# Cross attention and a three-way maxout layer: the order of work rewritten as three lists, with transposes by transfer, G in runs and a test of the sums

## The chip, the cores and the metric

The kernel runs on one core of a Trainium2 chip. The metric is the device time of one execution in microseconds (us). Three runs of the kernel before took 165.41, 166.38 and 168.26 us; their median is 166.38. The profile is of one execution, and its times are counted from its first instruction.

## The reference

`x` holds 8 batches of 8 heads, 512 rows and 64 columns; `state` has 32 rows for each batch and head. All inputs and the output are float32.

```python
scores  = softmax(x @ state.T / 8);  xread = scores @ state      # 512 rows per head
scores2 = softmax(state @ x.T / 8);  sread = scores2 @ x         # 32 rows per head
t = concat([xread, sread], axis=2)        # 544 rows per batch and head
t = t.transpose(0, 2, 1, 3).reshape(8 * 544, 512)                # heads side by side
h = max(t @ w1, t @ w2, t @ w3)           # w: 512 x 768
out = h @ w_out                           # 768 x 512
```

The reference takes each row's maximum off before the exponential. The softmax is the same without it as long as no exponential or sum leaves the range of the number type.

## The kernel before

Matmuls are in bf16 and sums in float32. `xread` is never formed. For each batch the kernel computes G, the product of the block of states and the weights (`g_cols`, L239, copied from PSUM at L245), so that layer 1 is `a @ G` (`x_maxout`, L260): `a` holds the softmax weights. G has 2,304 columns for each of two head parities, computed in six slices of 384, one per block `m` of 128 hidden columns.

Per batch the steps are these. `load_x` (L69) loads x on POOL's DMA queue and casts it to bf16. x is transposed on PE, 16 matmuls of 128 columns (`x_transpose`, L150, copied at L153), or by a DMA transpose on SyncE's queue (`x_transpose_dma`, L157). `scores` multiplies (L171) and takes the exponential on ACT (L176), with no maximum taken off. `softmax` sums (L183) and inverts (L185) on DVE and multiplies on POOL (L186). `a` is transposed on PE (`a_transpose`, L197, L198) or by a DMA (`a_transpose_dma`, L202). `sread` (L216) multiplies the same exponentials with x, 32 matmuls whose right side is 64 columns of x and 64 columns of ones that stand behind x, 128 columns in all, so that the sum of each row comes with the product; its result is transposed by a DMA (L224). Layer 1 makes three products per block (L260), copies the first on ACT (L264) and takes the maxima on DVE (L267, L268). Layer 2 (`ffn_out`, L285) makes four groups of 128 rows per batch; ACT copies each (L292) and POOL's or SyncE's queue stores two at a time (L301).

PSUM has two pools: four single banks (tag `pw`: three for each layer-1 group, one for each layer-2 group, and the transposes) and two double ones (tag `two`: slices of G and scores).

The order of each engine is the order in which the code is written; nothing reorders it. Batches 0 and 1 have a part written out by hand, with `keep_busy` matmuls (L116) while the first data come. From batch 2 on, `slots` attaches to each of the six layer-1 blocks of batch b the steps of batch b+1 and the layer-2 groups that are pending. x of batches 0 to 3 and `a` of batches 0 to 2 are transposed on PE; for later batches both are transposed by transfer, and x is loaded two batches before its layer 1.

Of the kernel before, what the change touches and what calls it, by code (L numbers as in the profile page):

```python
# [8 lines left out]
F32 = mybir.dt.float32  # L9
BF16 = mybir.dt.bfloat16  # L10
AX = mybir.AxisListType
AF = mybir.ActivationFunctionType


@with_exitstack
def kernel(
# [10 lines left out]

# [19 lines left out]
    wpool = ctx.enter_context(tc.tile_pool(name="weights", bufs=1))  # L50
# [3 lines left out]


    def load_st(k, eng):
        eng.dma_start(
            out=st_f[k],
            in_=state[2 * k:2 * k + 2].rearrange("b h n d -> (b h n) d").rearrange("(p t) d -> p t d", t=4))

    st_f = [data.tile([128, 4, D], F32, name=f"stf{k}") for k in range(B // 2)]
    load_st(0, nc.sync)


    x_sb = [data.tile([128, XW + D], BF16, name=f"x{b}") for b in range(B)]
    xv = [t[:, 0:XW].rearrange("p (h j d) -> p h j d", j=J, d=D) for t in x_sb]
# [6 lines left out]
    def x0_heads(g):  # L73
        return x[0].rearrange("(s g) (p j) d -> g p s (j d)", g=2, j=J)[g]

    x0_sb = x_sb[0][:, 0:XW].rearrange("p (s g jd) -> g p s jd", g=2, s=HS)
    x0_f = data.tile([128, HS, J * D], F32, name="x0f")
    nc.sync.dma_start(out=x0_f, in_=x0_heads(0))
    zero = const.tile([128, 512], BF16, name="zero")
    nc.vector.memset(zero, 0.0)  # L80
    ident = const.tile([128, 128], BF16, name="ident")
    make_identity(nc, ident)
    nc.gpsimd.dma_start(out=x0_sb[1], in_=x0_heads(1))
    for b in range(B):
        nc.gpsimd.memset(x_sb[b][:, XW:XW + D], 1.0)

    chunks = ((0, 1), (1, 3), (3, 6))
    w_sb = [wpool.tile([128, HS, 3, (m1 - m0) * 128], BF16, name=f"w{m0}") for m0, m1 in chunks]
    wout_sb = wpool.tile([128, NM, d_model], BF16, name="wout")

    def load_w(c):
        m0, m1 = chunks[c]
        for i, w in enumerate((moe_w1, moe_w2, moe_w3)):
            nc.gpsimd.dma_start(  # L94
                out=w_sb[c][:, :, i, :],
                in_=w.rearrange("(kk p) f -> p kk f", p=128)[:, :, m0 * 128:m1 * 128])

    def w_cols(m):
        c = [m0 <= m < m1 for m0, m1 in chunks].index(True)
        f = (m - chunks[c][0]) * 128  # L100
        return w_sb[c], slice(f, f + 128)

    load_w(0)
    bds = [data.tile([128, 2, H, 2, Ns], BF16, name=f"bd{k}") for k in range(B // 2)]
    nc.vector.memset(bds[0], 0.0)
    load_x(1)
    load_w(1)

    warm = const.tile([128, 1], F32, name="warm")
    nc.scalar.activation(out=warm, in_=zero[:, 0:1], func=AF.Exp, scale=1.0)  # L110
    ats = data.tile([128, B, HS, Ns], BF16, name="ats")

    def keep_busy(n):
        p = pp.tile([128, 1024], F32, tag="two", name="idle")
        for _ in range(n):
            nc.tensor.matmul(p[:, 0:512], zero[:, 0:128], zero, start=True, stop=True)  # L116

# [4 lines left out]
    st = [data.tile([128, 4, 2, D], BF16, name=f"st{k}") for k in range(B // 2)]  # L122

    def states_cast(k, cast):
        cast(out=st[k], in_=st_f[k].unsqueeze(2).to_broadcast((128, 4, 2, D)))

    def states(k, copy):

        p = pp.tile([128, 4, 128], BF16, tag="pw", bufs=4, name="pt")
        for t in range(4):  # L130
            nc.tensor.transpose(p[:, t, :], st[k][:, t].rearrange("p c d -> p (c d)"), ident)  # L131
        for c in range(2):
            r = slice(64 * c, 64 * c + 64)
            copy(out=bds[k][r, :, :, c, :].rearrange("p b h (q t) -> p (b h) q t", t=4),  # L134
                 in_=p[r].rearrange("p t (k q) -> p k q t", q=8))


    xT, e, a, aT, G, ht, osb = {}, {}, {}, {}, {}, {}, {}

    def new(d, b, shape, name, bufs=2):  # L140
        d[b] = work.tile(shape, BF16, tag=name, bufs=bufs, name=name)

    def x_transpose(b, g, copy):

        if g == 0:
            new(xT, b, [128, H, 2, 128], "xT")
        p = pp.tile([128, HS, 2, 128], BF16, tag="pw", bufs=4, name="pxt")
        for s in range(HS):
            for jj in range(2):
                nc.tensor.transpose(  # L150
                    p[:, s, jj, :],
                    xv[b][:, 2 * s + g, 2 * jj:2 * jj + 2, :].rearrange("p j d -> p (j d)"), ident)
        copy(out=xT[b].rearrange("p (s g) j t -> p g s j t", g=2)[:, g], in_=p)  # L153

    def x_transpose_dma(b):
        new(xT, b, [128, H, 2, 128], "xT")
        nc.sync.dma_start_transpose(out=xT[b].rearrange("p h j t -> p (h j) t"), in_=x_sb[b][:, 0:XW])  # L157

    def scores(b, g0, g1):
        n = g1 - g0  # L160
        if g0 == 0:
            new(e, b, [128, J, 2, HS, Ns], "e")
        if n == 2:
            p = pp.tile([128, J, n, HS, Ns], F32, tag="two", name="ps")
        else:
            p = pp.tile([128, J, n, HS, Ns], F32, tag="pw", bufs=4, name="psh")
        for jj in range(2):
            for g in range(g0, g1):
                for s in range(HS):
                    h = 2 * s + g  # L170
                    nc.tensor.matmul(  # L171
                        p[:, 2 * jj:2 * jj + 2, g - g0, s, :], xT[b][:, h, jj, :],
                        bd(b, h).rearrange("p c n -> p (c n)"),
                        start=(g == g0 and s == 0 and (n == 2 or jj == 0)),
                        stop=(g == g1 - 1 and s == HS - 1), skip_group_check=True)
        nc.scalar.activation(out=e[b][:, :, g0:g1], in_=p, func=AF.Exp, scale=scale)  # L176

    def softmax(b, g0, g1, mul):
        n = g1 - g0
        if g0 == 0:  # L180
            new(a, b, [128, J, 2, HS, Ns], "a")
        den = work.tile([128, J, n, HS], F32, tag=f"den{n}", name="den")
        nc.vector.reduce_sum(out=den, in_=e[b][:, :, g0:g1], axis=AX.X)  # L183
        rden = work.tile([128, J, n, HS], F32, tag=f"rden{n}", name="rden")
        nc.vector.reciprocal(out=rden, in_=den)  # L185
        mul(  # L186
            out=a[b][:, :, g0:g1].rearrange("p j g s n -> p j (g s) n"),
            in0=e[b][:, :, g0:g1].rearrange("p j g s n -> p j (g s) n"),
            in1=rden.rearrange("p j g s -> p j (g s)").unsqueeze(3).to_broadcast((128, J, n * HS, Ns)))

    def a_transpose(b, g, copy):

        if g == 0:
            new(aT, b, [128, J, 2, 128], "aT", bufs=3)
        p = pp.tile([128, J, 128], BF16, tag="pw", bufs=4, name="pat")
        for j in range(J):
            nc.tensor.transpose(p[:, j, :], a[b][:, j, g].rearrange("p s n -> p (s n)"), ident)  # L197
        copy(out=aT[b][:, :, g, :], in_=p)  # L198

    def a_transpose_dma(b):  # L200
# [4 lines left out]
    late = []  # L205

    def sread(b):

        p = pp.tile([128, 2, 2, D], F32, tag="pw", bufs=4, name="psr")
        for j in range(J):  # L210
            for g in range(2):
                for s in range(HS):
                    xj = xv[b][:, 2 * s + g, j, :]
                    both = bass.AP(xj.tensor, xj.offset,
                                   (xj.ap[0], (XW - ((2 * s + g) * J + j) * D, 2), (1, D)))
# [4 lines left out]
        rd = work.tile([128, 2, 1], F32, tag="rd", name="rd")  # L220
        nc.vector.reciprocal(out=rd, in_=p[:, :, 1, 0:1])
        sr = work.tile([128, 2, D], BF16, tag="sr", bufs=B, name="sr")
        nc.vector.tensor_mul(out=sr, in0=p[:, :, 0, :], in1=rd.to_broadcast((128, 2, D)))
        late.append(lambda: nc.sync.dma_start_transpose(  # L224
            out=ats[:, b].rearrange("p s n -> p (s n)"), in_=sr.rearrange("p g d -> p (g d)")))


    copies_due = []

    def g_cols(b, ms, copies=(nc.scalar.copy, nc.scalar.copy), defer=(False, False)):  # L230

        for m, copy, wait in zip(ms, copies, defer):
            if m == 0:
                new(G, b, [128, 2, NM * 384], "G", bufs=3)
            w, f = w_cols(m)
            p = pp.tile([128, 2, 512], F32, tag="two", name="pg")
            for s in range(HS):
                for g in range(2):
                    nc.tensor.matmul(  # L239
                        p[32 * s:32 * s + 32, g, 0:384].rearrange("p (i f) -> p i f", i=3),  # L240
                        bd(b, 2 * s + g)[64 * g:64 * g + 64, g, :], w[64 * g:64 * g + 64, s, :, f],
                        start=True, stop=True, tile_position=(64 * g, 32 * s))

            def place(m=m, p=p, copy=copy):
                copy(out=G[b][:, :, m * 384:(m + 1) * 384], in_=p[:, :, 0:384])  # L245

            if wait:
                copies_due.append(place)
            else:
                place()  # L250


    def maxout(b, m, n, lhs, rhs, nk):
        if m == 0:
            new(ht, b, [128, NM, n], "ht", bufs=4)
        pw = []
        for i in range(3):
# [196 lines left out]
```

## Time and profile before

| | |
|---|---|
| median of three runs | 166.38 us (165.41 to 168.26) |
| span of the profiled execution | 164.5 us |
| PE, weight loads, DVE, ACT, POOL busy | 149.7, 70.9, 96.0, 99.1, 44.0 us |
| first layer-1 matmul, end of the last matmul | 13.6, 160.3 us |
| layer 1 of x, 288 matmuls (L260) | 71.2 us |
| layer 2 (L285) | 47.9 us |
| copies of G on ACT (L245), 48 | 36.5 us, 0.805 each |
| copies of layer 1 on ACT (L264), 48 | 28.3 us, 0.590 each |
| maxima on DVE (L267, L268), 48 each | 32.6 and 33.0 us |

The profile gives the profiled execution's own time as its span alone; the three timed runs lie 0.9, 1.9 and 3.8 us above it. PE's busy time counts a modelled end for each matmul; sums of what groups occupy are lower than its column. In a line of the chain stand start, duration and what ran; in a line of groups, what is written and read, the count, the busy time and the mean in ns.

### The profile page before, as it was taken

Reading aid. Unit: us, or ns where it says so; the run is one execution under the profiler, and the core shown is the slowest. Engines: PE = TensorE matmul, PEld = TensorE weight load, DVE = VectorE, ACT = ScalarE, POOL = GpSimd, SP = SyncE. Lnnn points to the kernel's source line nnn. Section 1 sums busy time; section 2 is a strip of 40 time slices with the busy share of each in tenths; the row PEclk is TensorE's granted clock in tenths of the full one; section 3 lists DMA queues with packets and bytes.
Section 4 is the critical chain, followed back from the end, with each engine's and each line's share of the span. In section 5 each row is a group of like instructions: output and inputs, shape, how many; then the busy total and the mean of one; then the engine's idle time right before and its main releaser. Section 6 shows DMA issues by size and latency. Waiting matters only on the chain.

```text
span 164.5 us, 3569 instructions
## 1 busy us (share of the span) xinstructions
PE 149.7 (91%) x1432; PEld 70.9 (43%) x1449; DVE 96.0 (58%) x162; ACT 99.1 (60%) x158; POOL 44.0 (27%) x64
## 2 busy tenths in 40 slices
PE   7658699988999999999999999999999999999990
PEld 2425243533445444434344434444444466665430
DVE  4675777889418553665548464865586455585001
ACT  3355578366896678853876688648755853333440
POOL 8975550106150601081016101410141010100140
PEclk9999999999999999999999999999999999999999
DMA  4999999800039999269992989460306030030373
GB/s 132 195 174 199 204 200 248 122 7 0 0 120 130 144 256 198 53 116 145 277 193 87 133 187 104 162 191 14 128 0 195 8 130 0 0 132 0 128 235 148
DMA packets 31824, 20.94 MB, mean 127 GB/s; under 512 B 17184, under 2 KB 29344, under 8 KB 31808
## 3 DMA queue, kind: packets, MB, share of 16 engines
q0 software_dynamic: 15632, 15.08, 46.3%
q1 hardware_dynamic: 16176, 5.64, 18.5%
q8 instruction: 11, 0.18, 0.5%
q14 instruction: 5, 0.04, 0.1%
HBM read 15.20 MB, written 8.91 MB: 147 GB/s over the span
## 4 chain that ended last, share of the span: by engine, by line
PE 63%; DVE 11%; ACT 10%; DMA 6%; POOL 4%; issue 4%; DVEq 0%; ACTq 0%; POOLq 0%
PE pw L260 34%; PE po L285 20%; DMA x<-in_x_dram 4%; PE pg L239 4%; DVE den L183 4%; DVE t L267 3%; ACT e L176 3%; ACT G L245 3%; DVE ht L268 3%; PE ps L171 2%; ACT t L264 2%; PE psr L216 2%; POOL w L94 1%; DMA out_dram<-osb 1%; POOL a L186 1%
## 5 line engine op out<-in xcount | busy, mean ns | idle before, releaser
L260 PE MATMUL pw<-aT,G 128*128 128x512 bf16 x288 | 71.2, 379 | 3.6 <-ACT G L245 1.8
L267 DVE TENSOR_TENSOR t<-t,pw 128x512 bf16<-128x512 bf16 (+1 forms) x54 | 35.1, 650 | 41.6 <-ACT t L264 40.0
L285 PE MATMUL po<-wout,ht 128*128 128x512 bf16 x188 | 47.9, 380 | 0.8
L260 PEld LDWEIGHTS <-G 128*128 128x128 bf16 x288 | 26.7, 98 | 36.2 <-issue 5.1
L245 ACT CAST G<-pg 128x768 bf16<-128x768 f32 x48 | 36.5, 805 | 8.0 <-PE pg L239 7.6
L264 ACT CAST t<-pw 128x512 bf16<-128x512 f32 (+1 forms) x54 | 30.5, 566 | 14.1 <-PE pw L260 12.6
L268 DVE TENSOR_TENSOR ht<-t,pw 128x512 bf16<-128x512 bf16 (+1 forms) x54 | 35.5, 658 | 5.6
L292 ACT COPY osb<-po 128x512 f32<-128x512 f32 x33 | 19.4, 587 | 21.2 <-PE po L285 20.7
L285 PEld LDWEIGHTS <-ht 128*128 128x128 bf16 x204 | 18.4, 98 | 23.6 <-issue 4.7
L301 POOL DMA_DIRECT2D out_dram<-osb x14 | 7.8, 559 | 70.2 <-ACT osb L292 70.2
L186 POOL TENSOR_TENSOR a<-e,rden 128x1024 bf16<-128x1024 bf16 (+1 forms) x8 | 14.4, 1800 | 33.4 <-DVE rden L185 19.8
L239 PE MATMUL pg<-w,bd 64*32 64x384 bf16 x384 | 13.0, 328 | 1.1 <-DMA w<-in_moe_w_dram 1.1
L183 DVE TENSOR_REDUCE den<-e 128x32 f32<-128x1024 bf16 (+1 forms) x9 | 9.9, 1095 | 2.6 <-ACT e L176 2.6
L176 ACT ACTIVATE e<-ps 128x1024 bf16<-128x1024 f32 x7 | 7.2, 1024 | 5.8 <-PE ps L171 5.8
L260 PE MATMUL pw<-ats,w 128*128 128x256 bf16 x72 | 8.8, 273 | 0.0
L239 PEld LDWEIGHTS <-bd 64*32 64x32 bf16 x384 | 3.6, 89 | 11.7 <-issue 11.7
L260 PEld LDWEIGHTS <-w 128*128 128x128 bf16 x72 | 7.0, 98 | 2.1
L94 POOL DMA_DIRECT2D w<-in_moe_w_dram x9 | 6.8, 770 | 0.0
L69 POOL DMA_DIRECT2D x<-in_x_dram x7 | 6.7, 957 | 0.0
L150 PE MATMUL pxt<-ident,x 128*128 128x128 bf16 x64 | 4.4, 219 | 2.2 <-DMA x<-in_x_dram 1.1
L134 ACT COPY bd<-pt 64x512 bf16<-64x512 bf16 x6 | 3.5, 580 | 4.2 <-PE pt L131 4.1
L171 PEld LDWEIGHTS <-xT 128*128 128x128 bf16 x128 | 4.7, 98 | 2.4 <-DVE xT L153 0.8
(42 smaller groups left out, 63.4 us busy)
## 6 DMA issues: line engine op xcount, KB each, us to landing
out_dram<-osb POOLq DMA_DIRECT2D x14, 512.0 KB, 3.7
x<-in_x_dram POOLq DMA_DIRECT2D x7, 512.0 KB, 9.0
w<-in_moe_w_dram POOLq DMA_DIRECT2D x3, 384.0 KB, 10.3
w<-in_moe_w_dram POOLq DMA_DIRECT2D x3, 256.0 KB, 8.2
wout<-in_moe_w_out_dram POOLq DMA_DIRECT2D x1, 768.0 KB, 16.4
x0f<-in_x_dram SPq DMA_DIRECT2D x1, 512.0 KB, 4.0
out_dram<-osb SPq DMA_DIRECT2D x1, 512.0 KB, 2.7
out_dram<-osb SPq DMA_DIRECT2D x2, 256.0 KB, 2.2
```

Source lines behind the costliest of these rows:

```text
L94: nc.gpsimd.dma_start(out=w_sb[c][:, :, i, :], in_=w.rearrange("(kk p) f -> p kk f", p=128)[:, :, m0 * 128:m1 * 128])
L176: nc.scalar.activation(out=e[b][:, :, g0:g1], in_=p, func=AF.Exp, scale=scale)
L183: nc.vector.reduce_sum(out=den, in_=e[b][:, :, g0:g1], axis=AX.X)
L186: mul(out=a[b][:, :, g0:g1].rearrange("p j g s n -> p j (g s) n"), in0=e[b][:, :, g0:g1].rearrange("p j g s n -> p j (g s) n"), in1=rden.r ...
L239: nc.tensor.matmul(p[32 * s:32 * s + 32, g, 0:384].rearrange("p (i f) -> p i f", i=3), bd(b, 2 * s + g)[64 * g:64 * g + 64, g, :], w[64 * ...
L245: copy(out=G[b][:, :, m * 384:(m + 1) * 384], in_=p[:, :, 0:384])
L260: nc.tensor.matmul(p[:, 0:n], lhs(i, k), rhs(k), start=(k == 0), stop=(k == nk - 1))
L264: nc.scalar.copy(out=t0[:, 0:n], in_=pw[0][:, 0:n])
L267: nc.vector.tensor_max(t1[:, 0:n], t0[:, 0:n], pw[1][:, 0:n])
L268: nc.vector.tensor_max(ht[b][:, m, :], t1[:, 0:n], pw[2][:, 0:n])
L285: nc.tensor.matmul(p, ht[b][:, m, j * 128:(j + 1) * 128], wout_sb[:, m, :], start=(m == 0), stop=(m == NM - 1))
L292: nc.scalar.copy(out=o[:, j, :], in_=p)
```

## The change

Each step becomes a small function with a short name, and the order is three lists of such names: one for batches 0 to 2, one that is run for batches 2 to 6, and one for the rest. A number is a batch (in the second list relative to the round's), a letter the engine that copies or the queue (D DVE, A ACT, P POOL, S SyncE). `l1` is layer 1's matmuls, `m0` its copy, `m1` its maxima, `l2` layer 2, `l2c` its copy, `so` a store, `sc`, `ex`, `sum`, `wt` scores to softmax weights, `g`/`gc` a slice of G and its copy, `gr`/`grc` a run and its copy, `xtd`, `atd`, `srt` DMA transposes of x, `a` and the state read, `lx`, `lw`, `lst` loads.

- x of batches 2 to 7 and `a` of batches 2 to 7 are transposed by DMA on SyncE's queue; batches 0 and 1 stay on PE, and are begun together.
- G of batches 2 to 7 is computed in runs of 512 columns (one of 256), in G's own order of columns, instead of slices per block; weights are one tile, loaded in twelve pieces instead of nine.
- For batches 2 to 7 POOL copies x into a tile with a column of ones between heads (`pad`), and the state read takes 65 columns instead of 128.
- All sums are kept (`seen`). At the end DVE tests that they lie between 1e-18 and 1e18, a matmul adds up the answer over partitions, each engine reads it into a register and branches: if the test fails, all is computed again with the row maximum taken off. With the given inputs the branch goes past this code, which is 4,147 instructions long.
- The last layer-2 group is made in two halves of 256 columns, stored by SyncE's and ACT's queues; the states' rows are stored by two transfers instead of eight.

```diff
+FIRST = """
+    ident; clr 0; zero; lx 1; lst 0 A; lxg 0 1; busy 5; stc 0 D; busy 4; clr 3; lw 1 2 1; stt 0; lx0 S;
+    cx0 D; warm; xt 0 0; stp 0 A; xt 1 0; xtc 0 0 A; sc 0 0; lw 1 2 0; lw 0 1 1; xt 1 1; xones 0; ex 0 0;
+    xtc 1 0 D; sc 1 0; sum 0 0; xtc 1 1 A; xt 0 1; xtc 0 1 D; lw 1 2 2; lw 0 1 2; sc 0 1; sc 1 1; ex 1 0;
+    lw 0 1 0; ex 0 1; g 1 1; ex 1 1; lw 2 4 2; gc 1 1 A; lw 2 4 1; lst 1 A; g 0 0; wt 0 0 P; lw 2 4 0;
+    sum 1 0; wt 1 0 P; sum 0 1; wt 0 1 P; at 1 0; at 0 0; sum 1 1; lw 4 6 0; wt 1 1 D; gc 0 0 A; at 0 1;
+    atc 0 0 D; atc 0 1 D; g 1 0; g 0 1; atc 1 0 D; gc 1 0 A; stc 1 P; lw 4 6 1; xones 1; at 1 1; lw 4 6 2;
+    atc 1 1 A; clr 2; lx 2; l1 0 0; lst 2 P; l1 1 0; m0 0 0; gc 0 1 A; g 0 3; g 1 2; m0 1 0; l1 0 1; sr 0;
...
+    stt 3; srs 2; l1 1 5; l2 0 2; l2 0 0; m0 1 5; stp 3 A; gr 2 0 512; gr 2 1792 2304; gr 2 1024 1280;
+    sum 2 -; grc 2 1280 1792 A; xtd 3; l2 0 1; l2c 0 2 A; grc 2 1024 1280 A; l2c 0 1 A; stc 2 D; stt 2;
+    grc 2 512 1024 D; m1 1 5; grc 2 0 512 D; wt 2 - P; atd 2; l2c 0 0 D; so 0 2 4 A; grc 2 1792 2304 D;
+    stp 2 D; so 0 0 2 P;
+"""
+EACH = """
+    lx 2; sc 1 -; l1 0 0; l2 -1 2; l1 0 1; m0 0 0; l2 -1 0; l2c -1 2 A; xtd 2; gr 1 1024 1280; gr 1 0 512;
+    m1 0 0; m0 0 1; gr 1 512 1024; ex 1 -; l1 0 2; l2c -1 0 A; grc 1 1024 1280 A; m1 0 1; sum 1 -;
+    grc 1 512 1024 A; l2 -1 1; l1 0 3; m0 0 2; wt 1 - P; l1 0 4; atd 1; gr 1 1792 2304; l2c -1 1 A; m1 0 2;
+    pad 1; m0 0 3; grc 1 0 512 A; m0 0 4; gr 1 1280 1792; sr 1; m1 0 3; l2 -1 3; m1 0 4; l1 0 5;
+    grc 1 1792 2304 A; grc 1 1280 1792 A; srs 1; m0 0 5; l2c -1 3 D; m1 0 5; so -1 2 4 P; srt -2;
+    so -1 0 2 S;
+"""
+LAST = """
+    srt 5; srt 6; srt 7; l1 7 0; l1 7 1; l2 6 0; l2 6 1; m0 7 0; m0 7 1; m1 7 0; l1s 0; l1 7 3; m0 s 0;
...
+    l2c s 1 A; sos 1 S; l2c 7 3 A; l2 7 0; so 7 3 4 S; l2c 6 2 A; l2c 7 1 D; look; l2c 7 0 A; so 6 2 4 S;
+    so 7 0 2 S; l2 s 0; l2c s 0 A; sos 0 S; flag; l2p 7 2 0 256; l2p 7 2 256 512; l2pc 7 2 0 256 D;
+    l2pc 7 2 256 512 A; sop 7 2 0 256 S; sop 7 2 256 512 A;
+"""
...
+    def pad(b):
+        xp[b] = work.tile([128, HS, J, 2 * D + 2], BF16, tag="xp", name="xp")
+        nc.gpsimd.memset(xp[b][:, :, :, D:D + 1], 1.0)
+        v = xv[b].rearrange("p (s g) j d -> p g s j d", g=2)
+        for g in range(2):
+            nc.gpsimd.tensor_copy(out=xp[b][:, :, :, g * (D + 1):g * (D + 1) + D], in_=v[:, g])
...
+    def g_run(b, c0, c1):
+        new_g(b)
+        n = c1 - c0
+        if n > 256:
+            p = two_banks([128, 2, 512], F32, "pg")
+            ps = [p[:, g] for g in range(2)]
+        else:
+            p = None
+            ps = [bank([128, 512], F32, "pgh") for _ in range(2)]
+        g_mm(b, lambda s, g: ps[g][32 * s:32 * s + 32, 0:n],
+             lambda v: v.rearrange("p i f -> p (i f)")[:, c0:c1])
...
+    perform(FIRST)
+    for b in range(2, B - 1):
+        perform(EACH, b)
+    perform(LAST)
...
+    bad = nc.values_load(flag[0:1, 0:1], min_val=0, max_val=1,
+                         skip_runtime_bounds_check_because="flag is the result of a comparison")
+    with tc.If(bad != 0):
+        for b in range(B):
...
```

## The prediction

> **What bounds the kernel now.** I read the busy shares first, then the chain that ended last, then stretches of the span, last the DMA queues. Shares, clock, and the queue that loads instructions:
>
> ```profile
> PE 149.7 (91%) x1432; PEld 70.9 (43%) x1449; DVE 96.0 (58%) x162; ACT 99.1 (60%) x158; POOL 44.0 (27%) x64
> ...
> PEclk9999999999999999999999999999999999999999
> ...
> q8 instruction: 11, 0.18, 0.5%
> ```
>
> TensorE (PE) is busy for 91% at the full granted clock; VectorE (DVE) has 58%, ScalarE (ACT) 60%. PE's column shows modelled ends, so I take what a group occupies from the chain (start, duration, what):
>
> ```profile
> 12.70 1.07 PE pxt L150 x16
> ...
> 107.28 1.29 PE pw L260 x6
> 108.58 0.56 PE psr L216 x32
> ...
> 113.70 0.45 PE pg L239 x16
> ...
> 116.84 0.48 PE ps L171 x16
> ```
>
> So a layer-1 group (six 512-column matmuls) costs 1.29 us, as does a layer-2 group; 16 G matmuls 0.45, so a 384-column slice 0.225; the scores of a batch 0.48, its state read 0.56; 16 x transposes 1.07. The `a` transposes of a batch take 0.62, those of a state pair 0.33, a layer-1 group of the states (12 of 256 columns) 1.30, all from the same view. Whole kernel: 48x1.29 + 34x1.29 + 6x1.30 + 48x0.225 + 8x0.48 + 8x0.56 + 4x1.07 + 3x0.62 + 4x0.33 = 140.2 us. The first layer-1 starts at 13.6, after 3.8 us of that sum. From there PE needs 136.4 and ends at 160.3, in 146.7: **10.3 us of waits** are what a new order can win. Stretches (PE, weight load, DVE, ACT, POOL; clock; DMA share; GB/s) tell where:
>
> ```profile
> 30.00:47.00 17.00, 15.30 (x184) 6.92 (x184) 12.00 (x20) 11.47 (x18) 3.70 (x5) 1.00 0.11 16
> ...
> 100.70:116.80 16.10, 15.79 (x160) 6.84 (x159) 10.03 (x17) 10.88 (x17) 3.00 (x4) 1.00 0.46 106
> ...
> 131.70:160.30 28.60, 28.40 (x165) 16.26 (x166) 12.77 (x24) 11.23 (x23) 3.61 (x7) 1.00 0.25 89
> 160.30:164.50 4.20, 0.00 (x0) 0.00 (x0) 0.42 (x1) 0.37 (x1) 0.00 (x0) 1.00 0.40 149
> ```
>
> The steady round from 100.7 holds 15.3 us of matmul (36+24 at 0.215, 6 slices, scores, state read) in 16.1: 0.8 is lost. The last 28.6 are full. Most waits lie before 50.
>
> **PE's work after.** Four x transposes on PE become two, three `a` transposes two: minus 2.14 and 0.62. A state read of 65 columns instead of 128 I take at 0.35 (bounds: 0.28 by columns, 0.56 unchanged), six times. G of a batch keeps 2,304 columns in 5 runs instead of 6 slices: 1.3 against 1.35 (bounds 1.1, 1.6). The new list also does batch 1's scores and `a` transposes and four slices in all before its first layer-1. Behind that point stand 48+34 groups 105.8, states 7.8, eight slices 1.8, six batches' runs 7.8, six scores 2.9, reads 2x0.56+6x0.35 = 3.2, state pairs 1.0, the flag's matmul 0.1: **130.4**, against 136.4.
>
> **Where that starts.** Before layer-1 of batch 0 the new list wants x of batch 1 (512 KB as counted at the destination), half of x of batch 0 (256) and six weight pieces of 128: 1,536 KB through POOL's queue. Before, 1,152 KB had landed there at 12.65 (the chain's DMA step that ends in the 1.07 above) and 1,920 at 16.8 (PE's second wait on a weight load): 186 KB per us. 384 more take 2.1: 14.7, plus the slice's 0.36 and its eviction of 0.8 on ACT. **15.8**; bounds 13.6 (as now) and 17.5.
>
> **Waits of the first list: 3.5.** x of batch 2 stands behind all weights: 3,584 KB, the same sum as before, where it landed at 26.2 (issued 12.82, 13.4 to landing). Its DMA transpose, four before of 4.3 to 7.1 to landing, median 6.4, gives 32.6. The list puts 14.3 us of matmul between the first layer-1 and scores of batch 2, which is 30.1: 2.5 late. At its end, sums 1.23+0.35, the product on POOL 1.91 and the DMA transpose 4.2 (7.7 in all) stand before layer-1 of batch 2. DVE reaches those sums after eleven maxima pairs (1.38 each), two state placings and three reads, some 21.7 behind the start; PE comes to the layer-1 at 26.9+2.5. That is about even; I take 1.0 more.
>
> **Waits of the five rounds: 0.6 each, 3.0.** PE has 7.74+5.16+1.3+0.48+0.35 = 15.0. ACT has six copies of 0.59, four runs at 1.02 (nearest row: the exponential, 128x1024 from PSUM), two of 0.37, the exponential and three outputs: 11.2. DVE has six pairs, sums, read and an output: 11.0. Both fit, so only their order costs. The padded copy of x adds 2.4 on POOL per batch (POOL's cast of 128x512 takes 0.61, so 1,024 elements 1.15, twice). POOL has 27% busy, but the copy stands between the product and the state read; with product from about 8.0 to 9.9 it ends at 12.3, where PE wants it at 12.1. Nothing, then, or a few tenths. The store queued behind it on POOL comes later still.
>
> The tight part is SyncE's queue. In one round it transposes x of batch b+2, loaded in that same round, and behind it `a` of batch b+1, wanted by the next round's first layer-1. Before, x was loaded a transpose ahead, and still:
>
> ```profile
> SPq L157 <- DMA x<-in_x_dram: 7.0, 2, 3.5
> ```
>
> ```profile
> 72.04 0.96 POOL L69 DMA_DIRECT2D x<-in_x_dram  x1
> ...
> 89.44 0.96 POOL L69 DMA_DIRECT2D x<-in_x_dram  x1
> ```
>
> ```profile
> 81.03 3.61 SPq L157 DMA_TRANSPOSE xT<-x  x1
> ...
> 89.52 1.23 SPq L202 DMA_TRANSPOSE aT<-a  x1
> ...
> 98.55 2.35 SPq L157 DMA_TRANSPOSE xT<-x  x1
> ```
>
> From the load's issue to the transpose's 9.0 and 9.1 pass; the transpose holds the queue 2.4 to 3.6; aT lands 4.2 after its own issue (median; 3.0 to 7.6). The load follows on POOL the store of the last output copied, 14.9 behind the start of the round before. From there two rounds pass before aT is used: 2P = 14.9+9.05+3.0+4.2 = 31.2, P = 15.6. PE alone gives 15.0. I take **15.6**; bounds 15.0 and 16.5.
>
> **Last list and end.** Its 28.5 of matmul replaces 28.6, with 0.2 of waits; the sums' test is six small operations beside matmuls (0.1 on PE, counted). After PE's end 4.2 stays. The branch is new. Each engine reads a register and jumps past a fallback of 4,147 instructions, while the last store flies. No row shows a register read: from 0.2 (ACT's shortest instruction) to 2.1 (a store's landing). Instruction packets took 0.5% of 16x164.5 us for 11, 1.2 each. A fetch is then 1.2, or with a landing in front (1.7 to 2.1) up to 3.3. Issue 0.35 plus both, less the store's 2.1, is from nothing to 3.6; with 0.35, a read of 0.4 and a fetch of 2.9 it is **1.5**, nearest to the rows of DMA that fetches resemble.
>
> The Trainium skill, "Runtime: NRT & Kernel Launch", section "Instruction fetch mechanics", speaks against the change here: a taken branch whose target lies outside the current two-page window has to wait for a DMA fetch of that page. By it a fetch is certain; were the target already loaded, the sum would be 1.5 less. No row of before shows such a jump.
>
> **Sum.** 15.8 + 130.4 + 3.5 + 3.0 + 0.2 + 4.2 + 1.5 = 158.6 us of span against 164.5. The median of runs, 166.38, stands 1.9 above the span: **160.5 us**, 3.5% less.
>
> **Rivals.**
> (a) *The order wins all it could*: weights land as needed (14.5), 2.5 of waits in all, branch hidden: 14.5+130.4+2.5+4.2 = 151.6, a time of 153.5. For it: neither ACT nor DVE is full. Against: x of batch 2 lands no earlier.
> (b) *The waits come back elsewhere*, 10.3 as now instead of 6.7: 162.2, a time of 164.1, no measurable change. For it: four single-bank buffers must serve three banks per layer-1 group, and maxima (1.38 on DVE) follow 1.29 of matmul.
> (c) *Slower, by SyncE's queue.* If x takes 13.4 to land in the rounds, as it did once in the load-heavy start, instead of 9.0, then 2P = 35.5, P = 17.8, five rounds cost 11 more: 171.5. It decides from a landing of 11.5 on (P = 16.8, 5x1.2 = 6 more than forecast, the whole gain). For it: x, a store of 512 KB and a transpose share the DMA engines. Against: the loads at 72 and 89 met stores too and kept 9.0.
> (d) *The change does less than it says*: transposes by transfer for batches 2 and 3 are hidden anyway and padding saves nothing on PE (0.56 stays). That adds 1.3: 161.8, inside the forecast's range.
>
> **How the numbers follow.** Forecast with (d) 0.55 (157 to 163), (a) 0.15, (b) 0.20, (c) 0.10. The unknown costs span 150 to 169 if all fall on one side. For 8 in 10 the range reaches into (a) and past (b): 153.5 to 165.5. Before's own runs spread by 1.7%, so 2% (163.1 to 169.7) is about what can be told from no change. Faster: (a) and most of the forecast, 0.66; same 0.23, mainly (b); slower 0.11.
>
> **What would show it.** First layer-1 near 15.8; PE waiting for xT of batch 2 around 30; rounds between first layer-1s of batches 3 to 6 of 15.6; SyncE's queue waiting for x about 9 after each load; from the last copy to the end 4.9 instead of 3.3 us. The prediction is wrong if rounds take over 16.5, if ACT or DVE in order hold PE for more than 1 us a round, or if the jump costs over 3 us.

## The result, and the profile after

The kernel after takes 168.21 us (median of 16 runs) against 166.58 for the kernel before (16 runs beside it): a ratio of **1.011, 95% interval 1.008 to 1.014**. It is 1.1% slower where 3.5% faster was forecast, and above the range. Its profiled execution has a span of 165.3 us and an own time of 167.19; time minus span is 1.9, as assumed. A ratio here is taken over the undisturbed runs of both kernels and can differ from that of the two medians by up to 0.5%.

The end of the chain of waits of the kernel after (start, duration, what):

```profile
153.03 1.34 PE po L420 x12
...
154.40 0.37 ACT osb L424
```

PE ends at 154.4; 152.9 was predicted, and before it was 160.3. So the new order gave PE 5.9 us. But the span ends 10.9 later, where 4.2 + 1.5 = 5.7 was predicted. After the last copies, from 154.8 on, no engine computes; stretches of the kernel after (length, busy time of PE, weight load, DVE, ACT and POOL, granted clock, DMA share, GB/s):

```profile
10.00:20.00 10.00, 7.93 (x103) 5.32 (x101) 7.74 (x16) 6.25 (x10) 5.88 (x7) 0.67 1.49 181
...
154.80:165.30 10.50, 0.00 (x0) 0.00 (x0) 0.00 (x0) 0.00 (x0) 0.00 (x0) 0.58 0.33 102
```

The last row is 10.5 us at 102 GB/s; before, the 4.2 behind PE's end moved 149. The DMA issues from 150 on (queue, KB each, median us from issue to landing) show what is late: SyncE's last 128 KB take 9.1 us. Of the two stores of 256 KB one is the second store of states' rows, and for the states' stores the profile has no landing; the 5.4 is that of a layer-2 group that stands behind the first of them on the queue.

```profile
out_dram<-osb SPq DMA_DIRECT2D x2, 512.0 KB, 5.8
out_dram<-osb SPq DMA_DIRECT2D x2, 256.0 KB, 5.4
out_dram<-osb SPq DMA_DIRECT2D x1, 128.0 KB, 9.1
```

The same view of the kernel before, from 150 on:

```profile
out_dram<-osb SPq DMA_DIRECT2D x2, 256.0 KB, 2.2
out_dram<-osb SPq DMA_DIRECT2D x4, 64.0 KB, 2.1
out_dram<-osb POOLq DMA_DIRECT2D x4, 64.0 KB, 2.3
```

The other miss is the start. The first 20 us of the chain of the kernel after:

```profile
7.18 8.68 DMA w<-in_moe_w_dram
...
16.00 0.36 PE pg L324 x8
16.35 1.26 PE pat L265 x12
17.61 0.77 PE pg L324 x16
18.39 0.54 PE pat L265 x4
18.93 2.35 PE pw L376 x8
```

The weights land at 15.9, not 14.7. And behind the slice that they free stand, in PE's order, 2.57 us of `a` transposes and slices, which were thought to be done by then. Part of this runs at half the clock: PE rests 2.71 us for x until 9.53, and then 0.79, 0.22 and 1.07 us between 12.9 and 16.0; in stretches of 1 us the granted clock is 0.50 from 10 to 13 and from 17 to 20, which makes the mean of 0.67 above. PE's work in order of time (start, duration, what, in brackets the rest ahead of it):

```profile
9.53 0.83 PE L207 MATMUL pxt<-ident,x 128*128 128x128 bf16 x8 [2.71 <-DMA x<-in_x_dram]
```

Busy shares and the clock in 40 slices of the kernel after; the 6 and the 5 among the first five slices are that half clock:

```profile
PE 144.9 (88%) x1350; PEld 71.6 (43%) x1364; DVE 106.5 (64%) x182; ACT 88.4 (53%) x143; POOL 49.8 (30%) x65
...
PEclk9969599999999999999999999999999999999955
```

In the middle the change did what it says. The scores of batches 4 to 7 in the chain:

```profile
64.15 0.47 PE ps L232 x16
...
79.46 0.47 PE ps L232 x16
...
94.77 0.47 PE ps L232 x16
...
110.44 0.47 PE ps L232 x16
```

Rounds of 15.31, 15.31 and 15.67 us. The one before them, from the scores of batch 3 at 47.8, took 16.2, so the mean of the four is 15.6, as predicted. Of PE's time from the first layer-1 (18.7) to its end (154.4), 130.4 is work by the prediction's count; 5.3 is left for waits, where 6.7 was predicted.

### The profile page after: what moved, and what is told of

Read it like the earlier page. It is cut to its first block, busy times and chain, and to the rows that moved or that the text cites. A ratio compares the mean times of both kernels' runs of the same rounds, so it can differ in the third digit from the quotient of the medians.

```text
span 165.3 us, 3444 instructions
## 1 busy us (share of the span) xinstructions
PE 144.9 (88%) x1350; PEld 71.6 (43%) x1364; DVE 106.5 (64%) x182; ACT 88.4 (53%) x143; POOL 49.8 (30%) x65
## 4 chain that ended last, share of the span: by engine, by line
PE 75%; DVE 6%; DMA 5%; POOL 4%; issue 2%; ACT 1%; DVEq 0%; POOLq 0%
PE pw L376 39%; PE po L405 25%; DMA w<-in_moe_w_dram 5%; PE pg L324 5%; POOL w L151 2%; PE psr L297 2%; DVE t L397 2%; DVE ht L398 1%; DVE G L363 1%; PE ps L232 1%; DVE bd L198 1%; PE pat L265 1%; PE pgh L324 1%; PE po L420 1%; ACT t L391 1%
## 5 line engine op out<-in xcount | busy, mean ns | idle before, releaser
L405 PE MATMUL po<-wout,ht 128*128 128x512 bf16 x173 | 43.3, 379 | 1.2 <-DVE bd L198 0.7
L398 DVE TENSOR_TENSOR ht<-t,pw 128x512 bf16<-128x512 bf16 x48 | 33.0, 687 | 5.4 <-PE po L405 0.5
L412 ACT COPY osb<-po 128x512 f32<-128x512 f32 x24 | 14.0, 586 | 25.6 <-PE po L405 22.5
L363 ACT CAST G<-pg 128x1024 bf16<-128x1024 f32 x21 | 21.0, 1026 | 2.9 <-PE pg L324 2.9
L281 POOL COPY xp<-x 128x1024 bf16<-128x1024 bf16 x12 | 12.2, 1045 | 5.3 <-DMA x<-in_x_dram 5.3
L324 PE MATMUL pg<-w,bd 64*32 64x512 bf16 (+1 forms) x288 | 11.1, 373 | 1.3 <-DMA w<-in_moe_w_dram 1.3
L412 DVE COPY osb<-po 128x512 f32<-128x512 f32 x9 | 6.2, 688 | 8.3 <-PE po L405 8.3
L342 ACT CAST G<-pg 128x768 bf16<-128x768 f32 x12 | 9.5, 804 | 3.7 <-PE pg L324 3.7
L246 DVE TENSOR_REDUCE seen<-e 128x32 f32<-128x1024 bf16 (+1 forms) x10 | 9.9, 995 | 0.6 <-ACT e L239 0.6
L239 ACT ACTIVATE e<-ps 128x1024 bf16<-128x1024 f32 (+1 forms) x10 | 8.5, 864 | 3.4 <-PE ps L232 3.4
```

Of the source, the lines that this page charges most:

```text
L246: nc.vector.reduce_sum(out=den, in_=parity(e[b], g), axis=AX.X)
L281: nc.gpsimd.tensor_copy(out=xp[b][:, :, :, g * (D + 1):g * (D + 1) + D], in_=v[:, g])
L324: nc.tensor.matmul(p(s, g), bd(b, 2 * s + g)[64 * g:64 * g + 64, g, :], f(w_sb[64 * g:64 * g + 64, s]), start=True, stop=True, tile_positi ...
L363: copier[c](out=v, in_=p[:, :, 0:c1 - c0])
L398: nc.vector.tensor_max(ht[b][:, m, :], t1[:, 0:n], pw[2][:, 0:n])
L405: nc.tensor.matmul(p, ht[b][:, m, j * 128:(j + 1) * 128], wout_sb[:, m, :], start=(m == 0), stop=(m == NM - 1))
```

## The experiments: the end

Theory 2 says that the states' rows, now written by two transfers of 4 x 32 rows, are carried by four of the 16 DMA engines, and that the last store and the code fetches wait behind them. Theory 1 says that the far jump alone bounds the end. "Before" in what follows is the kernel before, run beside each on the same chip.

**Eight transfers again** (s8).

```diff
     def store_states(j, q):
-        queue[q].dma_start(
-            out=out.rearrange("(b t) f -> b t f", t=SP)[4 * j:4 * j + 4, S:SP, :],
-            in_=osb["s"][:, j, :])
+        for k in range(4 * j, 4 * j + 4):
+            (nc.sync if k % 4 < 2 else nc.gpsimd).dma_start(
+                out=out[k * SP + S:(k + 1) * SP, :],
+                in_=osb["s"][32 * (k % 4):32 * (k % 4) + 32, j, :])
```

> The changed kernel, but with the states' rows stored by eight transfers of 32 rows, as before the change, instead of two of 4x32 rows. Theory 1 (the far jump bounds the end: ScalarE resumes 6.7 us and VectorE 7.1 us after its branch, whatever the stores do): span 165 still, ScalarE's and VectorE's first instruction behind the branch near 162.5. Theory 2 (a transfer of 4x32 rows runs on four of the sixteen DMA engines, the last stores and the code fetches wait behind it there): the last store lands 2 to 4 us after its issue instead of 9.1, the resumption comes 3 to 4 us after the branch, span about 160.5, ratio to before about 0.985.

163.45 us, ratio 0.984 (0.981 to 0.987). This one edit turns the change from 1.1% slower to 1.6% faster. From the last copy to the end of the span it takes 5.5 us instead of 10.5. The issues from 150 on:

```profile
out_dram<-osb SPq DMA_DIRECT2D x4, 64.0 KB, 1.9
out_dram<-osb POOLq DMA_DIRECT2D x4, 64.0 KB, 2.3
out_dram<-osb SPq DMA_DIRECT2D x1, 256.0 KB, 2.5
out_dram<-osb SPq DMA_DIRECT2D x1, 128.0 KB, 3.7
```

The last store lands in 3.7 us instead of 9.1 and the layer-2 group's 256 KB in 2.5 instead of 5.4, beside the same jump. The spans differ by 3.5 and not by 5.0 because PE ended 1.6 later in this execution, in which its clock was at 0.50 for 10.2 us (11.0 to 21.2) instead of twice 3.4; whether that is all of the 1.6 is open. The ratios (1.011 and 0.984) put the store's shape at 4.5 us.

**The same edit on the kernel before** (bef_s2): its eight transfers become two, both on SyncE's queue.

> The kernel before, with one part of the change alone: each half of the states' rows is stored by one transfer of 4x32 rows on SyncE's queue instead of four of 32. Theory 2 (such a transfer is carried by four DMA engines): 64 rows of 2 KB at 0.084 us a packet and four of 16 engines are 2 x 2.7 = 5.4 us from about 159, and the last two stores' packets stand behind them on those engines: landing near 165.5, span 167, ratio 1.01 to 1.02. If the shape of the store costs nothing: span 164.5, ratio 1.00.

169.86 us, ratio 1.020 (1.013 to 1.027). From the last copy to the end 7.0 us pass instead of 3.3, with no branch in the kernel. SyncE's stores of 256 KB from 150 on are the two of states' rows, again without a landing, and two layer-2 groups, which landed after 6.5 us instead of 2.2:

```profile
out_dram<-osb SPq DMA_DIRECT2D x4, 256.0 KB, 6.5
```

So the loss needs no branch. This edit, like s8, also moves stores between the queues of SyncE and POOL; the next run keeps both queues.

**Four transfers of 2 x 32 rows** (s2x2): is it the size or the shape?

```diff
-        queue[q].dma_start(
-            out=out.rearrange("(b t) f -> b t f", t=SP)[4 * j:4 * j + 4, S:SP, :],
-            in_=osb["s"][:, j, :])
+        for k in (4 * j, 4 * j + 2):
+            (nc.sync if k % 4 < 2 else nc.gpsimd).dma_start(
+                out=out.rearrange("(b t) f -> b t f", t=SP)[k:k + 2, S:SP, :],
+                in_=osb["s"][32 * (k % 4):32 * (k % 4) + 64, j, :])
```

> The states' rows of layer 2 are stored by four transfers of 2 x 32 rows (128 KB each; the first of a pair on SyncE's queue, the second on POOL's), all else as in the kernel after. If a transfer is carried by as many DMA engines as its outermost count (4 x 32 by four: four completion marks per transfer were seen), a 2 x 32 transfer runs on two engines with 64 KB each, as long as a 4 x 32 one with 64 KB each: the time stays near the kernel after's, ratio 1.005 to 1.015, tail from the last copy to the end 9 to 11 us, two completion marks per transfer. If it is the size of the transfer (256 KB) and not its shape that holds the last stores, half the size gives most of what eight transfers gave: ratio 0.985 to 0.995, tail 5.5 to 7 us.

170.34 us, ratio 1.028 (1.019 to 1.036), with 12.6 us behind the last copy: half the size is no faster, even slower, and so it is not for want of POOL's queue that the two transfers are slow. From 150 on (in the second row the 11.2 is the landing of the last store; the states' store in it has none):

```profile
out_dram<-osb POOLq DMA_DIRECT2D x2, 128.0 KB, 9.3
...
out_dram<-osb SPq DMA_DIRECT2D x2, 128.0 KB, 11.2
```

The completion marks, packets of 4 bytes, are taken here to count the engines. Among the DMA packets of SyncE's queue behind 150 us there are 68 of them for six transfers (one issued a little earlier): four of 16 and two of 2. The kernel after has 72 for six, four of 16 and two of 4; with eight transfers it is 128 for eight, 16 each. The busy share of the 16 engines says the same: while a states' store of the new shape is the one that moves, SyncE's packets take 24.4% in the kernel after (150.0 to 151.5 us), 23.8% in bef_s2 (159 to 161) and 10.8% in s2x2 (150.5 to 152), that is 3.9, 3.8 and 1.7 engines. So the number of engines follows the outermost count of the transfer, 4, 2 or 32, and a store behind it on the queue waits. The Trainium skill has this rule: "DMA: Bandwidth & Descriptors", section "Why a DMA increments its semaphore by 16 and not by 1", says that a transfer runs on the largest number of engines up to 16 that divides the slowest dimension of both sides. Sixteen, four and two agree with the counts here. The prediction priced this edit at nothing without looking at it.

**Without the branch** (nb: the two-transfer store stays; nb_s8: with eight transfers). The register reads, the branch and the fallback are left out; the sums are still tested.

```diff
-    bad = nc.values_load(flag[0:1, 0:1], min_val=0, max_val=1,
-                         skip_runtime_bounds_check_because="flag is the result of a comparison")
-    with tc.If(bad != 0):
...
```

> The changed kernel without the read of the flag, the branch and the fallback behind it (the sums are still tested, nothing is done with the answer). Theory 1: the whole gain comes back, span 158.5 (154.8 + 3.3 + a little), ratio 0.97. Theory 2: the last store still lands at about 163, span 164 to 164.5, ratio 0.995 to 1.005.

> Both: no branch and fallback, and the states stored by eight transfers. Theories 1 and 2 agree on a span of 158 to 158.5 and a ratio near 0.965. With the two kernels beside it this gives the price of the jump with an unloaded DMA (s8 minus this), which theory 1 puts at 6, theory 2 at 2 to 3.

nb: 166.27 us, ratio 0.999 (0.995 to 1.004). nb_s8: 162.01 us, ratio 0.976 (0.974 to 0.978). From the last copy to the end 8.8 and 4.7 us. So the branch costs 0.8% or 1.3 us beside eight transfers, 1.2% or 1.9 us beside two; theory 1 accounts for the smaller part, and the store's shape for 2.7% with the branch and 2.3% without.

**A short fallback** (short: eight transfers, and of the fallback only layer 2 and the stores of the states' rows stay; the rest of it is left out, so the jump's target is near).

> The changed kernel with the states stored by eight transfers and a fallback of only its last step (layer 2 of the states and their stores; the rest of the fallback is left out), so that the jump is short; flag, register read and branch stay. If the price of the branch is the fetch of a far target: VectorE and ScalarE resume within 0.5 us of their branch, span 160.2 to 160.7, ratio 0.977 to 0.98. If it is the register read, the branch itself or the longer end: as with the whole fallback, span 161.8, ratio 0.984.

162.94 us, ratio 0.983 (0.974 to 0.992). The branch instructions of the kernel with eight transfers (duration in ns three times, start in us; `q` marks the sequencer of an engine):

```profile
L550 PEldq COMPARE_BRANCH  x1: 3554/3554/3554, 156.0 to 156.0; - x1
L550 DVEq COMPARE_BRANCH  x1: 72/72/72, 156.2 to 156.2; - x1
...
L550 DVEq EVENT_SEMAPHORE  x1: 21/21/21, 159.9 to 159.9; - x1
```

and those with the short fallback:

```profile
L550 PEldq COMPARE_BRANCH  x1: 350/350/350, 155.3 to 155.3; - x1
```

The fetch of a far target shows: on PE the branch takes 3,554 ns instead of 350, and DVE goes on 3.7 us behind its own. In the kernel after, where the slow stores occupy the DMA engines, DVE went on only after 7.1 us (155.0 to 162.1). But the end barely moved, 5.5 to 5.4 us behind the last copy; the last store's 3.7 us of landing run beside the fetch. The interval is too wide to tell this kernel from s8; how the branch's 1.3 us divide between register reads (0.47 to 0.87 us each with eight transfers) and a longer closing part stays open. The Trainium skill's rule on a taken branch ("Runtime: NRT & Kernel Launch", section "Instruction fetch mechanics"), that a target outside the two-page window is fetched before execution goes on, agrees with 3,554 against 350 ns.

**The third group of batch 6 stored earlier** (s8_tail).

```diff
-    ... m1 s 5; l2 s 1; l2c 6 3 A; l2 7 3; l2 7 1;
+    ... m1 s 5; l2 s 1; l2c 6 3 A; l2c 6 2 A; so 6 2 4 P; l2 7 3; l2 7 1;
```

The next line of the list loses the same copy and the store, which SyncE's queue had there.

> The kernel after with the states' rows stored by eight transfers of 32 rows, and in the last list the copy of the third layer-2 group of batch 6 and its store moved forward to the point where its matmuls have ended (behind the copy of the fourth), the store on POOL's queue and not SyncE's. If stores that still move at the end lengthen the tail even with eight transfers (the last store lands 3.7 us after its issue, against 2.2 in the kernel before), 0.5 to 1 us goes: ratio 0.978 to 0.981, tail 4.5 to 5. If the tail is now the jump's fetch, nothing changes: ratio 0.982 to 0.986.

163.50 us, ratio 0.982 (0.974 to 0.989); 5.5 us behind the last copy, as with s8. The last store still takes 3.7 us. So this store, at least, is not what holds the end once the shape is repaired.

## The experiments: the start

**Idle matmuls in the waits** (busy, with the two-transfer store; s8_busy, with eight).

```diff
-    cx0 D; warm; xt 0 0; stp 0 A; ...
+    cx0 D; warm; xt 0 0; busy 11; stp 0 A; ...
-    ... xt 0 1; xtc 0 1 D; ...
+    ... xt 0 1; busy 3; xtc 0 1 D; ...
-    ... lst 1 A; g 0 0; ...
+    ... lst 1 A; busy 4; g 0 0; ...
```

> The changed kernel with 18 more idle matmuls of zeros in the start (11 after the first x transposes, 3 before the scores of parity 1, 4 before the second slice of G), so that TensorE doesn't rest while x and the weights come. Theory 3 (TensorE's granted clock of 0.5 to 0.67 between 10 and 20 us is from its rests at 6.8 to 9.5 and 13 to 16, and costs some 2 us): the clock stays at 1.0 from 10 to 20, the first layer-1 comes at 17 to 17.5 instead of 18.7 and its group in 1.3 instead of 2.3, span 163. Rival (the first layer-1 is set by the weights' landing at 16.0 and the copies behind it, the clock costs nothing there): span 165 as now.

> The kernel after with eight transfers and the 18 idle matmuls in the start that held the granted clock at 1.0 there. If the first list is bound by data (x of batch 2 and its transposition, w_out), as the run with idle matmuls alone suggested, the first layer-1 comes 1 us earlier (17.7) and PE's end no earlier: ratio 0.982 to 0.988 against 0.984. If the lost clock was worth its 1 to 2 us and only the crowded end hid it, ratio 0.972 to 0.978.

busy: 168.13 us, ratio 1.014 (1.008 to 1.019). s8_busy: 163.67 us, ratio 0.988 (0.983 to 0.993). The stretch from 10 to 20 us of busy, columns as above:

```profile
10.00:20.00 10.00, 8.62 (x118) 5.00 (x117) 8.65 (x18) 7.30 (x12) 6.10 (x8) 1.00 1.55 187
```

The clock stays at 1.00 and the first layer-1 comes at 17.7 in both, instead of 18.7 (after) and 18.9 (s8). Still no gain shows, with the crowded end or without it. In busy the chain now goes through the data:

```profile
14.90 4.96 DMA stf<-in_state_dram
...
22.03 7.63 DMA x<-in_x_dram
...
31.84 8.94 DMA wout<-in_moe_w_out_dram
```

PE waits 0.52 us for the transpose of x of batch 2, then 1.62 for a maximum of DVE, which itself waited 2.50 for a load of states (0.56 in the kernel after), then 0.32 for `w_out`. Its layer 2 starts at 40.8, in the kernel after at 40.1. Theory 3, that the clock costs 2 us at the end, falls: in busy the microsecond is gained and spent on waits for transfers that came no earlier. In the profile of s8_busy PE ends 1.4 us before it does in that of s8, but this is the fastest of its four runs, and the ratios show no gain.

**POOL's loads earlier** (pool, with eight transfers): w_out and x of batch 3 are issued ahead of the padded copy of batch 2, which holds POOL until x of batch 2 has landed; the last weights and x of batch 2 are issued ahead of a cast of states. Theory 4 says that these held-up issues leave the DMA engines idle.

```diff
-    ... gc 1 0 A; stc 1 P; lw 4 6 1; ... clr 2; lx 2; l1 0 0; ...
+    ... gc 1 0 A; lw 4 6 1; ... clr 2; lx 2; stc 1 P; l1 0 0; ...
-    ... clr 1; pad 2; ... ones; lwo; g 1 4; ... m0 0 2; lx 3; m0 0 3; ...
+    ... clr 1; lwo; lx 3; pad 2; ... ones; g 1 4; ... m0 0 2; m0 0 3; ...
```

> The changed kernel with the states stored by eight transfers and POOL's order in the first list freed: the last weights and x of batch 2 are issued before the cast that waits for a state load, and w_out and x of batch 3 before the padded copy that waits for x of batch 2. Theory 4 (POOL's queue, held up by waiting computation, leaves the DMA engines idle at 20 to 22 and 28 to 31, and late data then hold TensorE until layer 2 begins): x of batch 2 lands before 27, w_out before 36, TensorE's end 1 to 2 us earlier, span 160 to 161, ratio 0.973 to 0.979. Rival (the first list is held by maxima and copies, not by data): span 161.8, ratio 0.984.

168.91 us, ratio 1.016 (1.007 to 1.024): 3.2% slower than s8. Its chain:

```profile
29.57 10.60 DMA xT<-x
...
40.21 1.04 PE ps L232 x16
```

The DMA transpose of x takes 10.6 us beside the two loads (512 and 768 KB), and scores of batch 2 start at 40.2 instead of 35.6, with a wait of 3.0 us for that transpose; 1.4 of the difference was there at the first layer-1 (20.3 instead of 18.9). Theory 4 has the sign wrong. A kernel with this order, the idle matmuls and the earlier store together (all):

> All of it with the branch kept: eight transfers for the states, POOL's order freed, 18 idle matmuls in the start, and the second store of batch 6 issued on POOL's queue some 2 us sooner. If theory 4 holds, the 1 us that the idle matmuls win at the first layer-1 now survives: span 158.5 to 159.5, ratio 0.965 to 0.97. If the first list is held by copies and maxima: as the kernel with eight transfers, 0.98 to 0.984.

166.14 us, ratio 1.000 (0.996 to 1.003): the wait for that transpose is there too (3.4 us).

**Without the padded copies** (s8_np2: eight transfers; POOL writes 64 columns of ones behind x, and the state read has 128 columns again).

```diff
-    x_sb = [data.tile([128, XW + (D if b < 2 else 0)], BF16, name=f"x{b}") for b in range(B)]
+    x_sb = [data.tile([128, XW + D], BF16, name=f"x{b}") for b in range(B)]
-    ... clr 1; pad 2; g 1 3; ...        (and "pad 1" in the rounds)
+    ... clr 1; xones 2; g 1 3; ...      (and "xones 1" in the rounds)
```

> The kernel after with the states' rows stored by eight transfers, and without the padded copies: for batches 2 to 7 POOL writes 64 columns of ones behind x as for batches 0 and 1, and the state read takes 128 columns again instead of 65. Against the same kernel with the padded copies (ratio 0.984): if PE's work sets the rounds, six reads of about 0.18 to 0.2 us more each lengthen PE's chain by 1.1 to 1.2 us: rounds of 15.5, ratio 0.990 to 0.993. If the two padded copies of 1.05 us on POOL hold PE in the rounds (product, copies and state read in a row), they go with no loss or a gain: rounds of 15.3 or less, ratio 0.976 to 0.985.

171.27 us, ratio 1.030 (1.022 to 1.037), 4.6% above s8: neither expectation. The rounds, from the scores in its chain, did as the first one says:

```profile
72.45 0.47 PE ps L232 x16
...
87.94 0.47 PE ps L232 x16
```

15.49 us instead of 15.31, the 0.18 by which its state read is longer (0.56 against 0.38). The rest came before the rounds. POOL's issues in the kernel s8 (start, duration, what, and in brackets its wait):

```profile
30.14 2.04 POOL L281 COPY xp<-x 128x1024 bf16<-128x1024 bf16 x2 [6.12 <-DMA x<-in_x_dram]
32.27 0.83 POOL L156 DMA_DIRECT2D wout<-in_moe_w_out_dram  x1
33.08 0.90 POOL L137 DMA_DIRECT2D x<-in_x_dram  x1
```

and without the padded copies:

```profile
24.43 0.86 POOL L156 DMA_DIRECT2D wout<-in_moe_w_out_dram  x1
25.24 0.93 POOL L137 DMA_DIRECT2D x<-in_x_dram  x1
```

With nothing in POOL's way the two loads leave 8 us earlier, into the transpose again, which holds SyncE's queue and then PE:

```profile
31.78 5.26 SPq L219 DMA_TRANSPOSE xT<-x  x1
```

```profile
31.78 9.76 DMA xT<-x
...
41.59 1.03 PE ps L232 x16
```

Issuing it takes 5.3 us instead of s8's 2.1, and scores of batch 2 come 5.9 later than in s8: PE waits 4.9 for the transpose, and the first layer-1 was 1.2 late already. Two different edits (pool, s8_np2) thus show the same: the padded copy's wait on POOL keeps the loads out of the transpose's way.

## Why the prediction was wrong

The span was to be 158.6 and is 165.3. The 6.7 divide into +2.9 in "Where that starts", -1.4 in the waits, and +5.2 in "Last list and end".

**The step that failed: "Last list and end".** It says "After PE's end 4.2 stays" and prices the branch, but gives no price to the states' two transfers, which stand in the same list ahead of the last stores. Without branch and with eight transfers 5.1 us pass from PE's end to the end of the span, 0.9 more than the 4.2; the branch adds 0.8 and the transfers' shape 5.0, which makes the 10.9. The ratios confirm the size: 4.5 us for the shape. The profile of before has landings of the eight small stores, 2.1 and 2.3 us, but no row of a 4 x 32 transfer, so this term should have been bounded. An estimate from the kernel after gives its size: the two transfers are 256 packets of 2,048 bytes, a packet took 0.084 us at the median, and on the same four engines that is 5.4 us. How long they took is not on record, as the profile has no landing for them.

**The branch's 1.5 held in its sum:** 1.3 us by the ratios beside eight transfers (1.9 beside two). Its terms were both larger (reads 0.47 to 0.87 instead of 0.4, a fetch of some 3.3 instead of 2.9), but so was the store that flies beside them, 3.7 instead of 2.1.

**"Where that starts" was mis-sized:** 18.7 instead of 15.8. Of this, 1.3 is the later landing of the weights and 1.5 the `a` transposes and slices that stand in PE's order behind the slice that waits; the prediction counted them as done before the first layer-1, but not as late as that slice. Half the clock made them longer (from the end of that slice to the first layer-1 2.4 us, in busy 1.5). The runs with idle matmuls show no gain at the end from the clock. What the data would allow was not tried.

**Right:** PE's work behind the start, with a state read of 0.38 against 0.35. **Right in size by luck: the rounds**, 15.6 in the mean. The prediction took its 15.6 from SyncE's queue, with 9.05 us for x and 4.2 for the transpose of `a`. In these rounds x landed after 6.4 to 7.1 us, the one landing of such a transpose on record there is 2.9, and PE waited for neither: it is busy for 15.1 to 15.4 us of each round, and its waits are 0.7 for a copy of states in the first and 0.3 for a maximum in the last. In s8_np2 0.18 more of PE's work made a round 0.18 longer, so it is PE's own work, which the prediction put at 15.0, that sets them. **Waits of the first list** came out smaller: x of batch 2 was transposed in time, its scores at 35.0, without a wait. That margin is thin, as pool and s8_np2 show.

**The rivals.** (a) fell: the first layer-1 came at 18.7 instead of 14.5, 5.3 us of waits were left instead of 2.5, and the branch was not hidden. (b) fell: waits went, they did not come back. (c), the only one with the right sign, had the wrong mechanism: SyncE's queue did wait 66.4 us for x, five times,

```profile
SPq L219 <- DMA x<-in_x_dram: 66.4, 5, 27.8
```

but x landed in 7.1 us (median; the rival needed 11.5), and PE had no need of it in that time. (d) fell with s8_np2: the narrow read saves its 0.18 per batch.

With the store mended the forecast's own remainder is visible: s8 takes 163.45, 3 us above 160.5, and that is the start. It is ahead of both kernels, and no other version with the branch and the whole fallback is clearly faster (s8_tail 0.982, s8_busy 0.988).

## What to carry to other kernels

Price every transfer whose shape changes, also where fewer and larger ones look like a saving: here two transfers with an outermost count of 4 cost 4.5 us against eight with 32. Transfers ahead of the last store count at the end even when all engines have finished their work. Before an issue is moved earlier, or a copy ahead of it removed, look at what is then in flight beside the next DMA transpose.

## What the runs showed of the hardware

- The number of DMA engines that carry a store from SyncE's queue follows its outermost count: 16, 4 and 2 completion marks for 32, 4 and 2, and a busy share of 24% and 11% of the 16 engines for 4 and 2.
- A far taken branch takes 3.6 us on PE (s8, after) against 0.35 for a near one (short); DVE resumes 3.7 us behind its branch in s8, and after 7.1 in the kernel after, beside the slow stores.
- A DMA transpose of 128 x 2,048 elements that landed 4.4 us after its issue in s8 (6.4 in short) took 9.8 (s8_np2) and 10.6 us (pool) beside two loads of 1,280 KB in all.
- In the kernel after PE's granted clock went to 0.50 for 3.4 us behind a rest of 2.71 us (9.8 to 13.2), and again for 3.4 behind three rests of 2.1 us in all, within 3.1 (16.6 to 20.0); in s8, with a rest of 2.90 and two of 0.79 and 0.71, it stayed at 0.50 from 11.0 to 21.2. With 18 idle matmuls in the rests it stayed at 1.00. The Trainium skill, "TensorE: Matmul & The Clock Gate", section "Part 1: The HAM clock gate (the "warmup" mystery)", gives half the clock after at least one idle window of about 3.4 us; the trace agrees in the half, while the rests here were shorter.
